# Attention by quads of heads in four column strips, with DMA transposes and engine orders planned at build time

## The chip, the cores and the metric

One core of a Trainium2 chip. The metric is device time in microseconds (us). Times are medians of several executions. Chips differ a little, so versions are compared by their ratio to the kernel before on the same chip.

## The reference, cut to what matters

```python
scores = scale * q @ k.T                      # 8 batches, 12 heads, 448 tokens, 64 wide
e = exp(scores - m)
attn = e / (sum(e) + exp(-m))                 # softmax with one more 1 in the sum
x = (attn @ v), heads side by side            # 3584 tokens x 768
h = x @ w_in                                  # 768 -> 2048, the first GEMM
g = (a0 + a1*h + a2*h^2 + a3*h^3) / (1 + |b0||h| + |b1|h^2)
out = g @ w_out                               # 2048 -> 768, the second GEMM
```

Both kernels drop the maximum `m`: the scores are small, and exp(s)/(sum exp(s) + 1) is the same number.

## The kernel before

Tokens are split 3 x 128 + 64. Heads go in pairs: a score matmul uses 64 of the 128 rows of the array, two heads beside each other; sums use 64 of 128 columns. The last 64 tokens of both heads share zero-padded blocks (`kblk`, `vblk`, `oblk`) and full-array matmuls. PE (the matmul engine) transposes q and k.

```python
def transpose_pair(b, p):                     # 8 PE transposes for a pair of heads
    for j in range(NC):
        nc.tensor.transpose(tp[:, S + j*128:S + (j+1)*128], k3[:, j, hs, :], ident)
    nc.tensor.transpose(tp[:, S + SM:S + SM + 128], kblk[b % 2][:, p, :], ident)
    # ... the same for q
    nc.vector.tensor_copy(out=qk, in_=tp)

def attend(b, p):
    for j in range(NC):                       # denominators: two strips of 64 columns
        for hh in range(2):
            r = slice(64 * hh, 64 * hh + 64)
            nc.tensor.matmul(out=den[r, 0:S], lhsT=ones, rhs=e[j][:, hh, :], ...)
    nc.tensor.matmul(out=den[:, 0:S], lhsT=oblk, rhs=e[NC], ...)   # the rest, full array
    # ... u, the numerators, in the same way from v3 and vblk

# program order: one list of work units, sorted by hand-set times
for _, f, args in sorted(work, key=lambda w: w[0]):
    f(*args)
```

A tile scheduler then adds the waits. `gemm1` and `gemm2` use the full array.

The softmax here doesn't subtract the row's maximum and nothing guards it: scores larger than these inputs give would overflow.

## Time and profile before

| | before |
|---|---|
| median time | 557.6 us (3 runs), 556.8 (4 runs beside the change) |
| profiled span | 554.7 us |
| PE, DVE, ACT busy | 502.6, 393.4, 307.9 us |
| matmuls, changes of tile shape | 3056, 528 |

DVE is the vector engine, ACT the scalar engine, POOL the GpSimd engine, which here also issues the loads; SP issues stores. A line of a view by stretches gives a stretch, its length, and the busy time and count of each engine. A timeline line gives a start, a length, an engine, a source line, the operation, and in brackets how long the engine was idle before and what ended that.

### The profile page before, as it was taken

The numbers are of one execution on the slowest core, as the hardware profiler recorded it, in microseconds if no ns is written. First come the engines' busy times: TensorE is split into PE (matmuls) and PEld (weight loads), VectorE is DVE, ScalarE is ACT, GpSimd is POOL, SyncE is SP. The second block draws the span as 40 slices with busy tenths as digits, with TensorE's granted clock in tenths as the row PEclk, the third lists the DMA queues.
The fourth block names the chain that finished last, engine by engine and source line by source line (L and its number), as shares of the span: only waits on it lengthen the run. The fifth ranks groups of instructions, "written<-read, shape, count | busy, mean of one in ns | idle before, by whom it ended". The sixth has DMA issues, their size and how long they took to land.

```text
span 554.7 us, 7452 instructions
## 1 busy us (share of the span) xinstructions
PE 502.6 (91%) x3056; PEld 237.0 (43%) x3056; DVE 393.4 (71%) x576; ACT 307.9 (56%) x353; POOL 114.2 (21%) x140
## 2 busy tenths in 40 slices
PE   2983899899999999999999999999999999877886
PEld 0331344344444444444444444444544444443443
DVE  1120399998777868778777878778777868888741
ACT  0772488867565765656565765656574765322220
POOL 9963524300610014100610014100000000000000
PEclk9987799999999999999999999999999999998899
DMA  6999999920955019510965019510000000100012
GB/s 49 81 178 172 203 174 85 95 19 30 73 59 76 30 34 97 78 28 30 70 64 75 30 33 96 79 29 30 3 27 30 30 28 30 30 28 0 30 70 73
DMA packets 113633, 34.30 MB, mean 62 GB/s; under 512 B 107200, under 2 KB 109248, under 8 KB 113600
## 3 DMA queue, kind: packets, MB, share of 16 engines
q0 software_dynamic: 109216, 22.81, 47.7%
q1 hardware_dynamic: 4384, 11.02, 5.5%
q8 instruction: 24, 0.39, 0.3%
q14 instruction: 9, 0.07, 0.0%
HBM read 45.62 MB, written 11.01 MB: 102 GB/s over the span
## 4 chain that ended last, share of the span: by engine, by line
PE 59%; DVE 27%; DMA 5%; POOL 5%; issue 2%; ACT 1%; POOLq 0%
PE hp L217 22%; PE op L277 19%; PE sps L160 5%; DVE n L247 4%; PE u L192 4%; DMA k_152<-in_k_dram 4%; DVE h L223 3%; DVE c L239 3%; DVE n L245 3%; DVE n L248 3%; DVE w L237 3%; DVE c L241 3%; PE den L183 2%; PE u L196 2%; DMA q_151<-in_q_dram 1%
## 5 line engine op out<-in xcount | busy, mean ns | idle before, releaser
L165 ACT ACTIVATE e<-sps 128x896 f16<-128x896 f32 x144 | 130.1, 916 | 144.5 <-PE sps L160 142.2
L217 PE MATMUL hp<-xt,w_in_sb 128*128 128x448 f16 x768 | 168.2, 356 | 9.9 <-DVE osb L282 5.2
L277 PE MATMUL op<-w_out_sb,g 128*128 128x384 f16 x768 | 134.5, 330 | 6.3 <-DVE h L223 3.6
L223 DVE CAST h<-hp 128x448 f16<-128x448 f32 x128 | 78.9, 621 | 45.0 <-PE hp L217 45.0
L217 PEld LDWEIGHTS <-w_in_sb 128*128 128x128 f16 x768 | 71.7, 98 | 82.5 <-issue 27.8
L277 PEld LDWEIGHTS <-g 128*128 128x128 f16 x768 | 75.2, 99 | 61.6 <-issue 10.8
L242 ACT ACTIVATE c<-c,oneeps_c 128x1792 f16<-128x1792 f16 x32 | 57.1, 1784 | 48.2 <-DVE c L241 48.1
L282 DVE COPY osb<-op 128x384 f32<-128x384 f32 x56 | 31.0, 554 | 47.4 <-PE op L277 47.3
L151 DVE COPY qk<-tp 128x960 f16<-128x960 f16 x48 | 31.1, 652 | 37.5 <-PE tp L149 37.4
L160 PE MATMUL sps<-qk 64*128 64x448 f16 x288 | 53.0, 369 | 1.8 <-DVE qk L151 1.4
L243 ACT ACTIVATE c<-c 128x1792 f16<-128x1792 f16 x32 | 54.2, 1693 | 0.2
L183 PE MATMUL den<-e,ones 128*64 128x448 f16 x288 | 43.0, 368 | 2.1 <-ACT e L165 2.1
L205 DVE TENSOR_TENSOR xt<-u,rden 128x448 f16<-128x448 f32 x48 | 29.8, 621 | 20.0 <-ACT rden L202 17.4
L200 ACT ACTIVATE lden<-den,one_c 128x448 f32<-128x448 f32 x48 | 30.6, 637 | 10.5 <-PE den L187 10.3
L251 DVE TENSOR_TENSOR g<-n,c 128x1792 f16<-128x1792 f16 x32 | 34.7, 1086 | 2.1 <-ACT c L243 2.0
L172 ACT ACTIVATE er<-sps 128x448 f16<-128x448 f32 x48 | 26.1, 543 | 18.0 <-PE sps L167 18.0
L241 DVE TENSOR_TENSOR c<-c,w 128x1792 f16<-128x1792 f16 x32 | 34.7, 1084 | 0.0
L247 DVE TENSOR_TENSOR n<-n,h 128x1792 f16<-128x1792 f16 x32 | 34.6, 1083 | 0.0
L249 DVE TENSOR_TENSOR n<-n,h 128x1792 f16<-128x1792 f16 x32 | 34.6, 1081 | 0.0
L160 PEld LDWEIGHTS <-qk 64*128 64x128 f16 x288 | 13.1, 94 | 40.8 <-issue 38.6
L202 ACT ACTIVATE rden<-lden 128x448 f32<-128x448 f32 x48 | 27.8, 580 | 0.9
L270 POOL COPY gx<-g 128x1024 f16<-128x1024 f16 x4 | 4.2, 1043 | 116.4 <-DVE g L251 116.4
(146 smaller groups left out, 493.9 us busy)
## 6 DMA issues: line engine op xcount, KB each, us to landing
out_dram<-osb SPq DMA_DIRECT2D x24, 384.0 KB, 2.3
w_in_sb<-in_moe_w_in_dram POOLq DMA_DIRECT2D x1, 3072.0 KB, 19.7
w_out_sb<-in_moe_w_out_dram POOLq DMA_DIRECT2D x1, 3072.0 KB, 21.4
out_dram<-osb SPq DMA_DIRECT2D x8, 192.0 KB, 2.7
k_111<-in_k_dram POOLq DMA_DIRECT2D x9, 64.0 KB, 3.2
q_109<-in_q_dram POOLq DMA_DIRECT2D x9, 64.0 KB, 3.2
v_112<-in_v_dram POOLq DMA_DIRECT2D x3, 192.0 KB, 4.2
k_152<-in_k_dram POOLq DMA_DIRECT2D x3, 192.0 KB, 20.9
```

The source lines that it names most:

```text
L160: nc.tensor.matmul(out=sps[:, hh, 0:S], lhsT=qk[r, S + j * 128:S + (j + 1) * 128], rhs=qk[r, 0:S], start=True, stop=True,)
L165: nc.scalar.activation(out=e, in_=sps[:, :, 0:S], func=AF.Exp, scale=scale)
L183: nc.tensor.matmul(out=den[r, 0:S], lhsT=ones, rhs=e[j][:, hh, :], start=(j == 0), stop=False, skip_group_check=True,)
L217: nc.tensor.matmul(out=hp[:, 0:S], lhsT=w_in_sb[:, c, fc * 128:(fc + 1) * 128], rhs=xt[:, c, :], start=(c == 0), stop=(c == NDC - 1),)
L223: nc.vector.tensor_copy(out=hts[b][:, fc % FG, :], in_=hp[:, 0:S])
L241: nc.vector.tensor_tensor(out=c, in0=c, in1=w, op=ALU.mult)
L242: nc.scalar.activation(out=c, in_=c, func=AF.Ln, bias=oneeps_c)
L243: nc.scalar.activation(out=c, in_=c, func=AF.Exp, scale=-1.0)
L247: nc.vector.tensor_tensor(out=n, in0=n, in1=h, op=ALU.mult)
L249: nc.vector.tensor_tensor(out=n, in0=n, in1=h, op=ALU.mult)
L251: nc.vector.tensor_tensor(out=gs[b][:, gi * FG:(gi + 1) * FG, :], in0=n, in1=c, op=ALU.mult)
L277: nc.tensor.matmul(out=op[:, 0:HD], lhsT=lhs(fc), rhs=w_out_sb[:, fc, nh * HD:(nh + 1) * HD], start=(fc == 0), stop=(fc == NFC - 1),)
```

## The change

Its intent is to take work and hand-overs off PE. 448 tokens become 4 x 112, so that no remainder is left; four heads are summed side by side in strips of 32 columns; q and k of batches 1 to 7 are reordered by POOL and transposed by DMA; the output copies move from DVE to ACT; and every engine's order comes from a simulation in the kernel's own build, which picks the next operation by readiness and rank. The diff's core:

```diff
+LAT = {"PE": 0.3, "ACT": 0.2, "DVE": 0.2, "POOL": 0.2, "SP": 2.5, "DMA": 3.5}
+class Plan:                                   # ... ready(), slot(), run(): list scheduling
+        if e == "PE" and op.name[0] != self.mode:
+            op.end += 0.095
...
+    plan = Plan({
+        "PE": ("tr", "att", "mm"),
+        "ACT": ("head", "den", "acast", "osb", "e", "rat"),
+        "DVE": ("head", "cpt", "mult", "cast", "wc", "ng"),
+        "POOL": ("load",  "perm", "gx"),       # rank: loads before reorders
+        "SP": ("x", "out"),
+    })
+    PER = 4.1                                  # us a beat of two score pairs
+    T0 = 30.0                                  # from beat 12 on
...
+        def tiles(unit, half, lhs):            # sums: four strips of 32 columns
+            for j in range(J):
+                for i in range(4):
+                    nc.tensor.matmul(
+                        out=gen[unit["slot"]][32 * i:32 * i + 32, half, 0:S],
+                        lhsT=lhs(i, j), rhs=e_sb[m % NE][:, i % 2, :], ...)
...
+            def emit(src=src, mid=mid):        # POOL reorders, then SP transposes
+                    nc.gpsimd.tensor_copy(out=mid[0].bitcast(U32)[:, pr], in_=...)
+            def emit_x(mid=mid, dst=dst):
+                nc.sync.dma_start_transpose(out=dst[n % NK]..., in_=mid[0]...)
...
-    for _, f, args in sorted(work, key=lambda w: w[0]):
-        f(*args)
+    plan.run(due)
+    for op in plan.order:
+        op.emit()
```

## The prediction

> **What bounds the kernel now.** I read the page first: busy shares, then the 40 slices.
>
> ```profile
> PE 502.6 (91%) x3056; PEld 237.0 (43%) x3056; DVE 393.4 (71%) x576; ACT 307.9 (56%) x353; POOL 114.2 (21%) x140
> ...
> PE   2983899899999999999999999999999999877886
> ```
>
> PE is busy from a tenth of the span on, and no other engine is above 71%. But matmuls overlap, so a busy PE need not be one that streams data all the time. The second view is busy time by stretch (per row: length, then busy us and count of PE, PEld, DVE, ACT, POOL, then clock, DMA share, GB/s):
>
> ```profile
> 0.00:60.00 60.00, 34.68 (x194) 11.67 (x194) 9.52 (x22) 26.03 (x38) 44.62 (x64) 0.87 1.27 125
> 60.00:100.00 40.00, 38.06 (x239) 16.15 (x238) 32.36 (x46) 31.99 (x39) 15.39 (x17) 0.97 1.48 149
> 100.00:480.00 380.00, 371.35 (x2311) 177.27 (x2309) 306.21 (x444) 235.97 (x270) 52.12 (x57) 1.00 0.40 46
> 480.00:555.00 75.00, 58.54 (x318) 31.87 (x316) 45.35 (x66) 13.94 (x8) 2.08 (x2) 0.94 0.12 43
> ```
>
> There are three regimes: a start of 60 us in which PE waits for loads, 380 us at full clock with PE 98% busy, and a tail of 75 us with about 16 us of PE gaps. What PE does while "98% busy" is in the timeline of one steady stretch (start, length, engine, line, count); I read the distances between starts:
>
> ```profile
> 206.40 0.36 PE L160 MATMUL sps<-qk 64*128 64x448 f16 x2
> 206.70 1.31 PE L217 MATMUL hp<-xt,w_in_sb 128*128 128x448 f16 x6
> 207.84 0.35 PE L167 MATMUL sps<-qk 128*128 128x448 f16 x1
> 208.03 2.76 PE L277 MATMUL op<-w_out_sb,g 128*128 128x384 f16 x16
> 210.63 1.30 PE L217 MATMUL hp<-xt,w_in_sb 128*128 128x448 f16 x6
> 211.86 0.36 PE L160 MATMUL sps<-qk 64*128 64x448 f16 x2
> ```
>
> Six first-GEMM matmuls take 207.84-206.70 = 1.14 us, 0.19 each. Sixteen of the second GEMM take 2.60 us, 0.163 each. A 64-row pair costs as much as one full matmul, so its halves overlap; but from its start to the next 128-row one are 0.30 us, not 0.19: **each change of tile shape costs about 0.10 us**. From a full matmul to another full one (207.84 to 208.03) there is none. I took the median of all start distances in 100 to 480 us: 0.189 us within the first GEMM, 0.163 within the second, 0.285 from the first GEMM to scores, 4 ns inside a pair. That makes a change 0.096 us. For the attention sums:
>
> ```profile
> 104.86 0.76 PE L192 MATMUL u<-e,v_153 128*64 128x448 f16 x6
> 105.55 0.36 PE L196 MATMUL u<-er,vblk_86 128*128 128x448 f16 x1
> ```
>
> Six matmuls, two strips of 64 columns side by side, take 0.69 us with one change: (0.69-0.10)/3 = 0.197 us a step.
>
> Over the whole trace this closes. Streaming: first GEMM 768 x 0.189 = 145.2; second 896 x 0.163 = 146.0; full and half-array attention matmuls and transposes 131; together 422 us. The program order has 528 changes of tile shape: 51 us. Waits: 70 us, of which 29 in the first 60 us, 21 in the 380 steady us, 15 in the tail, the rest between 60 and 100. First matmul at 6.7 us, 5 us after the last. So PE's own sequence bounds 85% of the time; 131 + 51 us of it are attention and switching.
>
> **What the Trainium skill says.**
> - "TensorEngine Tiling (Array Packing)", Key Properties: changing the tiling mode drains TensorE. The trace agrees: 0.285 against 0.189 us.
> - "TensorE: Matmul & The Clock Gate", Part 3, Measured speedup vs the span model: a pack of tiles takes about one matmul plus 4 ns a tile, and three column strips were measured 2.38 times as fast. The trace shows the 4 ns between two 64-column strips; no run yet shows four.
> - "DMA: Bandwidth & Descriptors", Specifications: below 512 B a transfer misses line rate. The page counts 107200 of 113633 packets under 512 B.
> - "SBUF — State Buffer", Who interferes with whom: VectorE and GpSimd can lock each other out of a shared port. The trace fits: one rational step (L248) averages 0.733 us, but 0.60 in the tail, where GpSimd is idle.
>
> **The change, part by part.**
>
> PE. (a) The 448 tokens become 4 x 112, so the 64-token remainder with its zero-padded blocks goes. Scores: 24 quads x 8 row pairs = 192 x 0.193 = 37 us (before 144 pairs and 48 full ones, the same). (b) Denominator and numerator go in four 32-column strips: 1152 matmuls, 288 steps x 0.197 = 56.7 us; before 288 steps plus 96 full matmuls x 0.189 = 75. Gain 18 us, as no step carries zeros. (c) Transposes: 384 on PE become 96 for batch 0, about 4 us; before about 19, gain about 15 us. (d) The GEMMs are unchanged: 145.2 + 146.0. (e) Changes of tile shape, counted in the instruction order of the built program: 237 instead of 528, so 22.8 us instead of 51. Sum 37+56.7+4+291.2+22.8 = **412 us**, against 473: 61 us off the bounding engine.
>
> ACT. Durations from these rows:
>
> ```profile
> L165 ACT ACTIVATE e<-sps 128x896 f16<-128x896 f32 x144 | 130.1, 916 | 144.5 <-PE sps L160 142.2
> L223 DVE CAST h<-hp 128x448 f16<-128x448 f32 x128 | 78.9, 621 | 45.0 <-PE hp L217 45.0
> L200 ACT ACTIVATE lden<-den,one_c 128x448 f32<-128x448 f32 x48 | 30.6, 637 | 10.5 <-PE den L187 10.3
> ```
>
> 192 exponentials x 0.916 = 176; 24 x (0.637+0.580) = 29 instead of 58; rational 32 x (1.784+1.693) = 111; output copies move here, 28 x about 0.81 (768 elements, between 0.543 at 448 and 0.916 at 896) = 23; four casts, 4. Sum 343 us instead of 308.
>
> DVE. 60 casts of 896 at about 1.09 (0.621 plus 448 more at the slope of 0.554 to 0.621 from 384 to 448) = 65; 24 multiplies x 1.09 = 26; the rational 32 x 7.92 (sum of its nine rows) = 253; batch 0's copies 5. Sum 350 instead of 393: output and transpose copies leave it.
>
> Both lie beside PE, at about 78% of a 450 us span, so they matter by latency only.
>
> DMA and POOL. Loads are 1 KB runs, not 256 B. POOL gains 42 reorder steps, two copies each, about 46 us (from the gx copy's 1.04 us); SP gains 42 transposes of 229 KB. Both are asked for some 30 us early in the program, so hidden.
>
> Path at the start. With POOL's first memsets and small loads gone, I put the first exponential at 10.5 us (before 14.0). Batch 0 is then ACT-bound: 24 x 0.916 + 3 x 1.22 = 25.6 us, then 2 us for the last quad: first GEMM at about 38 us, before at 60. Until then PE does transposes, scores, sums, about 19.5 us. So 38 + (412-19.5) = 430.5 us if PE never waits again. To that, chosen rather than read: 3 us while batch 1's attention limits PE; 7 us in the steady part (before: 21 in 380; fixed planned orders and fewer hand-overs take most); 5 us in the tail (before 15):
>
> ```profile
> 527.39 1.80 ACT c L242
> 529.22 1.71 ACT c L243
> 530.95 1.10 DVE g L251
> ...
> 532.10 17.25 PE op L277 x104
> ```
>
> This serial rational of the last group remains, but the plan puts a tile of the batch before ahead of it and half the casts on ACT. Then 4.5 us for the last copy and store. Span 450; the measured time was 2.9 us over the span: **453 us**.
>
> **The rivals.**
> 1. *The strips do not overlap.* Four strips halve the weight width and double weight loads per step (8 instructions in 0.2 us instead of 4). If a step took 0.25 us: 15 us more, 468; if strips ran only in pairs: 57 more, 510. For: no run shows four. Against: two show a 4 ns offset, the plan allows 0.77 us for 16.
> 2. *The fixed order turns jitter into waits.* Each engine runs a plan made with constants; a slow step, such as DVE locked out by POOL's 46 us of new copies, holds all behind it. Against: DVE and ACT keep 20% slack. At the old steady 5.6% of waits: 14 us more, 467.
> 3. *A new wait for the transposes.* If reorder plus DMA transpose took over 30 us, scores would wait each quad; 5 us each over 21 quads is 100 us. Against: steady DMA share is 0.40.
> 4. *PE is no longer the bound.* Then nothing under about 343 us counts; ACT and DVE are too far away.
> 5. *Better than I chose:* no steady waits and a first GEMM at 30 us gives about 437.
>
> **Range and chances.** Rivals 1 and 2 in mild form reach 475, rival 5 sets 438. Faster by over 2% means under 546.4 us; only rival 3, or 1 and 2 at their worst together, gets there: 0.96, 0.03, 0.01.
>
> **What would show each step.** PE start distances: 0.19 us per four-strip step, 0.10 at changes; the PE stream from the first GEMM to the end; first GEMM near 38 us; ACT busy near 343, DVE near 350; score matmuls waiting for an SP transpose would show rival 3; PE gaps ended by DVE or ACT above 7 us in the steady part rival 2. The prediction is wrong if a four-strip step exceeds 0.25 us, or if PE waits over 45 us in all.

## The result and the profile after

483.5 us (481.3 to 486.4, 4 runs) against 556.8 for the kernel before on that chip: ratio 0.8685 (95% interval 0.8639 to 0.8732). A ratio is the mean time of one kernel's fast runs over that of the other's of the same rounds, so it is not quite the ratio of the medians. Faster, as forecast; but 30 us slower than the 453 predicted and outside the range (438 to 475).

The page after, busy shares and the slices of PE:

```profile
PE 433.8 (90%) x3296; PEld 210.0 (44%) x3296; DVE 335.0 (70%) x389; ACT 319.8 (67%) x337; POOL 123.0 (26%) x186
...
PE   3873977897998999999999999999999999998985
```

PE is at 90% again, of a shorter span; its holes lie in the first ten slices, about 120 us. By stretches (start, then to 100 us, steady part, tail):

```profile
0.00:60.00 60.00, 39.29 (x353) 18.36 (x354) 14.11 (x28) 31.47 (x39) 30.56 (x53) 0.91 1.22 181
60.00:100.00 40.00, 32.33 (x258) 13.40 (x256) 30.05 (x34) 31.90 (x35) 17.80 (x23) 0.87 0.94 130
100.00:380.00 280.00, 271.02 (x2104) 128.12 (x2103) 222.75 (x250) 209.88 (x223) 72.29 (x108) 1.00 0.52 84
380.00:480.00 100.00, 91.12 (x587) 50.15 (x584) 68.14 (x80) 46.51 (x42) 2.35 (x2) 0.99 0.15 44
```

From 60 to 100 us PE is now busy for 32 of 40 us, where before it was 38, and the clock granted is 0.87. A piece of the steady part, to be set beside the timeline of before:

```profile
252.08 0.82 PE L569 MATMUL gen<-w_out,g 128*128 128x384 f16 x4
252.83 1.70 PE L417 MATMUL gen<-e,vn 112*32 112x448 f16 x32
254.46 0.82 PE L569 MATMUL gen<-w_out,g 128*128 128x384 f16 x4
255.22 0.59 PE L391 MATMUL sps<-qt,kt 64*112 64x448 f16 x4
255.74 3.42 PE L569 MATMUL gen<-w_out,g 128*128 128x384 f16 x20
```

The 32 numerator matmuls of a quad take 254.46-252.83 = 1.63 us with the change of shape after them: eight steps of four at 0.19 us. Two score pairs take 0.52, with one change.

**Where the time went.** I split every start distance between matmuls into streaming (the durations of the prediction), 0.096 us where the tile shape changes, and the rest, called waits, in which slow clock is included.

| us | before | after | predicted after |
|---|---|---|---|
| streaming | 422 | 388 | 389 |
| changes of shape (528, 237) | 51 | 23 | 23 |
| waits, with the time ahead of the first matmul and after the last | 82 | 69 | 38 |
| span | 555 | 480 | 450 |

Of the 75 us gained in the span, 34 are streaming, 28 changes of shape and 13 waits. PE's work is as predicted to within 2 us, and the error is in the waits. For streaming this agreement is partly by construction, as the split takes the prediction's durations. What checks them are the medians of start distances in the steady part: 0.189 us in the first GEMM, 0.163 in the second, 0.19 per four-strip step, mostly 0.093 to 0.096 more at a change of shape. One term is missed: the second score pair of a block starts 0.23 us after the first, not 0.193; 56 such pairs in the steady part are 2 us, counted as waits here.

| waits, us | predicted | measured |
|---|---|---|
| up to the first GEMM (forecast at 38, seen at 46.6) | 18.5 | 30.2 |
| from there to 100 us (batch 1's attention) | 3 | 16.1 |
| steady part, 100 to 380 us | 7 | 13.6 |
| tail, and after the last matmul | 9.5 | 8.7 |

What PE stood at is in the timeline of PE, and in its waits summed by cause (who <- whom: us in all, times, longest):

```profile
35.75 1.87 PE L417 MATMUL gen<-e,vn 112*32 112x448 f16 x32
45.68 1.00 PE L391 MATMUL sps<-qt,kt 64*112 64x448 f16 x4 [8.05 <-DMA qt<-qp]
46.61 1.30 PE L481 MATMUL gen<-x,w_in 128*128 128x448 f16 x3
```

```profile
PE sps L391 <- DMA qt<-qp: 11.0, 2, 8.1
```

Batch 0's attention is over by 37.6 us. PE then stands 8.05 us for the first DMA-transposed queries. The first GEMM, whose input DVE has finished by 38.8 us, has its place in the order behind those scores. The issuing queues in the same stretch:

```profile
29.95 0.70 POOL L282 DMA_DIRECT2D w_in<-in_moe_w_in_dram  x1 [0.52 <-DMA w_in<-in_moe_w_in_dram]
...
30.65 0.74 POOL L345 COPY kp<-kn 112x256 uint32<-112x256 uint32 x2
...
31.33 0.74 POOL L345 COPY qp<-qn 112x256 uint32<-112x256 uint32 x2
31.42 1.32 SPq L351 DMA_TRANSPOSE kt<-kp  x1
...
32.80 4.65 SPq L351 DMA_TRANSPOSE qt<-qp  x1
```

The reorder of batch 1's first keys comes right after the last of twelve weight loads in POOL's queue, at 30.65 us, though the trace has these keys landed at 22.3. The transposes are issued at 31.4 and 32.8 and land at 41.8 and 45.6, ten and thirteen us later, while weights are in flight. The view of the tile `qt` gives the range (smallest, median, largest):

```profile
DMA to landing us min/median/max: 3.0/3.5/17.0
```

The 17 us are those of the second queries, issued at 46.5 us beside the second GEMM's weights; the plan takes 2.5 us for every transpose.

### The profile page after: what moved, and what is told of

Same layout as the page of the kernel before. It is cut to its first block, busy times and chain, and to the rows that moved or that the text cites. A ratio compares the mean times of both kernels' runs of the same rounds, so it can differ in the third digit from the quotient of the medians.

```text
span 479.5 us, 7892 instructions
## 1 busy us (share of the span) xinstructions
PE 433.8 (90%) x3296; PEld 210.0 (44%) x3296; DVE 335.0 (70%) x389; ACT 319.8 (67%) x337; POOL 123.0 (26%) x186
## 4 chain that ended last, share of the span: by engine, by line
PE 58%; DVE 15%; ACT 11%; DMA 10%; issue 4%; POOL 1%; DVEq 0%; POOLq 0%; ACTq 0%
PE gen L569 24%; PE gen L481 19%; PE gen L417 8%; PE sps L391 6%; ACT e L397 5%; DMA w_in<-in_moe_w_in_dram 4%; DMA qt<-qp 4%; DVE h L498 3%; DVE g L519 3%; DVE n L515 2%; ACT c L533 2%; DMA kt<-kp 2%; DVE n L519 2%; DVE c L519 2%; ACT c L530 1%
## 5 line engine op out<-in xcount | busy, mean ns | idle before, releaser
L397 ACT ACTIVATE e<-sps 112x896 f16<-112x896 f32 x192 | 166.5, 922 | 83.5 <-PE sps L391 82.9
L481 PE MATMUL gen<-x,w_in 128*128 128x448 f16 x768 | 161.3, 357 | 3.8 <-ACT o L579 1.5
L569 PE MATMUL gen<-w_out,g 128*128 128x384 f16 x768 | 134.2, 326 | 2.7 <-DVE g L519 2.3
L481 PEld LDWEIGHTS <-w_in 128*128 128x128 f16 x768 | 71.3, 98 | 83.4 <-issue 25.4
L498 DVE CAST h<-gen 128x896 f16<-128x896 f32 x60 | 64.9, 1086 | 49.5 <-PE gen L481 48.8
L391 PE MATMUL sps<-qt,kt 64*112 64x448 f16 x384 | 65.0, 395 | 21.2 <-DMA qt<-qp 11.0
L438 DVE TENSOR_TENSOR x<-gen,lden 128x896 f16<-128x896 f32 x24 | 26.1, 1086 | 35.7 <-PE gen L417 35.7
L519 DVE TENSOR_TENSOR g<-n,c 128x1792 f16<-128x1792 f16 x32 | 35.0, 1095 | 21.2 <-ACT c L533 20.5
L515 DVE TENSOR_SCALAR n<-n,abc 128x1792 f16<-128x1792 f16 x64 | 45.2, 706 | 1.2
L417 PE MATMUL gen<-e,vn 112*32 112x448 f16 x768 | 43.1, 368 | 1.0 <-ACT lden L430 0.9
L345 POOL COPY qp<-qn 112x256 uint32<-112x256 uint32 x42 | 27.6, 686 | 14.7 <-DMA qt<-qp 12.2
## 6 DMA issues: line engine op xcount, KB each, us to landing
w_out<-in_moe_w_out_dram POOLq DMA_DIRECT2D x4, 768.0 KB, 20.1
```

What stands on the lines that cost most here:

```text
L345: nc.gpsimd.tensor_copy(out=mid[0].bitcast(U32)[:, pr], in_=src[n % NN].bitcast(U32)[:, 2 * pr:2 * pr + 2] .rearrange("p e j d -> p j e d"))
L391: nc.tensor.matmul(out=sps[m % NS][0:P, hh, 0:S], lhsT=kt[n % NK][r, pr, j, :], rhs=qt[n % NK][r, pr].rearrange("p j c -> p (j c)"), start ...
L397: nc.scalar.activation(out=e_sb[m % NE], in_=sps[m % NS][0:P, :, 0:S], func=AF.Exp, scale=scale)
L417: nc.tensor.matmul(out=gen[unit["slot"]][32 * i:32 * i + 32, half, 0:S], lhsT=lhs(i, j), rhs=e_sb[m % NE][:, i % 2, :], start=(j == 0), st ...
L438: nc.vector.tensor_tensor(out=x_sb[b % NX][:, 2 * qd:2 * qd + 2, :], in0=gen[un_u["slot"]][:, :, 0:S], in1=r, op=ALU.mult)
L481: nc.tensor.matmul(out=gen[unit["slot"]][:, f // 2, 0:S], lhsT=w_in_sb[gi][:, c // 2, c % 2, (fc % FG) * 128:(fc % FG + 1) * 128], rhs=x_s ...
```

## The experiments

**Theory.** The loss at the start is the DMA transposes: reordered late, landing late behind weight loads, and, as orders are fixed, ready GEMM work standing behind them. **Rivals**: ACT's pace or the loads would set the start anyway; the low clock after the long wait is the loss; the plan's own pace holds attention back. In the table, spans and first GEMMs (us from the span's start) are of the profiled runs; the ratios are to the kernel before in the same rounds. Only pe_b1, wout_late and plan_knows ran on the control's chip. The change itself had ratios of 0.8685 and 0.8644, which the intervals allow, so differences across chips are sure to about 2 us only. Executions of one kernel differ by up to 5 us in span (479.5 to 484.6 for the change), so small differences are read from ratios.

| run | edit | ratio (95%) | span, us | first GEMM |
|---|---|---|---|---|
| change itself, again | none | 0.8644 (0.8613 to 0.8674) | 479.7 | 47.9 |
| pe_b1 | batch 1 transposed on PE | 0.8500 (0.8471 to 0.8529) | 473.1 | 40.5 |
| wout_late | second weights later | 0.8622 (0.8594 to 0.8650) | 475.9 | 48.0 |
| plan_knows | plan told of 11 us | 0.8571 (0.8543 to 0.8598) | 475.9 | 41.1 |
| wout_perm | wout_late, reorders first | 0.8510 (0.8471 to 0.8550) | 468.9 | 39.9 |
| warm | needless matmuls in the wait | 0.8648 (0.8612 to 0.8684) | 480.9 | - |
| pace_only | faster pace | 0.8548 (0.8514 to 0.8581) | 475.3 | - |
| pace | wout_perm and faster pace | 0.8251 (0.8221 to 0.8282) | 459.2 | 40.4 |
| pace_win | pace, other order of loads | 0.8251 (0.8226 to 0.8276) | 459.6 | - |
| all_pe | all transposes on PE | 0.9103 (0.9066 to 0.9140) | 504.1 | - |
| more_changes | 214 more changes of shape | 0.8979 (0.8942 to 0.9015) | 497.3 | - |
| more_full | its control | 0.8739 (0.8704 to 0.8774) | 485.3 | - |
| strips_serial | strips head by head | one run | 483.1 | - |
| extra_one | 12 more matmuls in one strip | one run | 525.6 | - |
| extra_spread | the same over four strips | one run | 487.5 | - |

All results were correct. A dash: not listed.

### The start: the control, batch 1 on PE, later weights, a plan that knows

> The changed kernel itself, for comparison on this chip. Both theories: 0.868 of the kernel before, span about 479.5 us, PE waits of 8 us and 3 us for transposed queries near 38 to 46 us and near 61 to 64 us.

As expected: 482.1 us, with waits of 8.6 and 3.5 us for the transposed queries.

```diff
-        if b == 0:
+        if b <= 1:
             transpose_by_pe(n)
```

> Batch 1 is transposed on PE too, so its score matmuls wait for no DMA transpose behind the weights. Theory A (late DMA transposes at the start cost about 15 us, through two waits, a lowered clock and attention that falls behind): the waits near 38 and 61 us go, the first GEMM starts near 38 us instead of 46.6, PE gains 4 to 5 us of work, the span falls to 466 to 472 us. Theory B (the start is bound by ACT's pace and by loads anyway): the first GEMM still starts after 44 us and the span stays at 480 us or grows by the 4 us.

473.9 us, span 6.6 us down although PE got more to do; the first GEMM at 40.5. The waits for DMA transposes are gone from PE. So they bound the start, not ACT's pace or the loads of weights. The profiled span is 1 us above the 466 to 472 expected (the four executions: 470.6 to 473.1): PE now stands 6.6 us, up to 77.5, for a DVE cast, so something else holds the stretch after 60 us.

```diff
+            if n in (7, 8):                   # in attention(n), after loads(n)
+                for cg in (2 * n - 14, 2 * n - 13):
+                    w_out_ops.append(w_out_op(cg))
-    w_out_ops = [w_out_op(cg) for cg in range(NG)]
+    w_out_ops = []
```

> The 3 MB of the second GEMM's weights are asked for some 20 to 35 us later, after the loads of quads 7 and 8. Theory A: transposes issued from 42 us on land in about 5 us instead of 12 to 17, the second wait goes and the first shrinks by 2 to 4 us; span 470 to 475 us. Theory B: 479 us as before.

480.3 us; the ratio lies inside the interval of the control, so no gain is shown. In the traces the second pair of transposes now lands in 4.4 and 6.6 us instead of 12.5 and 17, and the wait near 63 us is gone, but the first pair still lands at 42.9 and 47.0. It is issued beside the first weights, and the first GEMM stays at 48.0. PE stands 5.0 us for transposes instead of 12.1, but batch 0 ends later (see the section on the clock); what took up the rest is not shown.

```diff
+SLOW = ("xk3", "xq3", "xk4", "xq4", "xk5")
-            t = max(t, d.land if d.land else d.end + LAT[d.eng])
+            lat = 11.0 if d.name in SLOW else LAT[d.eng]
+            t = max(t, d.land if d.land else d.end + lat)
```

> Nothing is moved in memory; only the plan is told that the first five transposes land 11 us after issue instead of 2.5, so that PE's order puts first-GEMM matmuls ahead of the late scores. Theory A': the harm is done by the fixed order (GEMM work that is ready stands behind scores that are not); first GEMM near 38 us, span 469 to 473 us. Rival: the late transposes themselves delay batch 1's attention, ACT then paces it, and the order gains at most 3 us: 476 us or more.

477.6 us, ratio 0.0073 under the control's: 4 us. The first GEMM moves to 41.1 us as the theory says, but PE then stands 7.3 us at 65.7, at the next late transpose. The span, 475.9, is at the rival's 476. The order alone recovers 4 of the 8 us that pe_b1 gains on the same chip, so the fixed order is a part of the loss and the lateness itself another; the runs do not rank them.

### Both ends of the queue: later weights and earlier reorders

```diff
-        "POOL": ("load",  "perm", "gx"),
+        "POOL": ("perm", "load", "gx"),
```

(with the edit of the later second weights)

> The later second weights of the earlier run, and besides GpSimd's reorder copies go ahead of the loads that are still waiting in its queue, so that the first transposes are issued near 24 us instead of 31. Theory A (the transposes come late because reorder and transpose stand behind weight loads): the first pair lands before 37 us, no score waits over 2 us for it, first GEMM near 39 us, span 468 to 471 us, as far down as with batch 1 transposed on PE less its 5 us of PE work. Rival (only taking the transposes off DMA helps): a wait of over 4 us stays, span 475 us.

473.0 us, span 468.9, within the theory's 468 to 471, the first GEMM at 39.9. The first keys' transpose is issued at 23.9 us instead of 31.4. It still takes 10.8 us and the queries' 14 us, so they are not faster, only asked for sooner (the expected landing before 37 us holds for the keys, 34.6, not for the queries, 39.3). What is left of PE's wait for them:

```profile
PE sps L394 <- DMA qt<-qp: 1.8, 1, 1.8
```

This is as good as taking batch 1 off DMA (0.8510 against 0.8500), without its 5 us of PE work.

### The clock

```diff
+                    if m == 24:               # ahead of the score that waits
+                        for d in range(40):
+                            nc.tensor.matmul(out=sps[m % NS][:, 0, 0:S], ...)
```

> 40 needless full matmuls (their result is overwritten at once) are put in front of the score that waits 8 us for its transpose, so PE does not sit idle there and the granted clock stays up. If the lowered clock after the wait (0.74 in 40 to 60 us) is worth what the slow matmuls after it show, nine at about 0.4 instead of 0.19 us and two score pairs, the span falls by 2 to 3 us from 479.7. Rival: the clock is most of the loss; over 6 us. Or the matmuls only add themselves: no gain.

483.0 us: no gain, as the last of the three readings has it. The Trainium skill, in "TensorE: Matmul & The Clock Gate", Part 1, says that an idle window of about 3.4 us brings the clock down to half. The trace of the change agrees: 8 us without work, then half the clock from 40.8 to 51.0 us (0.74 on average over 40 to 60). But its clock is at half once more from 88.6 to 95.4 us, and in the 3.4 us before that PE never stood for more than 0.41 us, each time for an exponential; it was busy for 1.84 of the 3.4 us. So here a half-busy stretch was enough.

The needless matmuls did keep the clock up (1.00 over 40 to 60 us). From the late score to the 24 matmuls of the first GEMM 8.57 us pass instead of the control's 9.81, so the low clock after this wait is worth about 1 us. The waits up to 60 us fell from about 25 to 19 us, but the extra matmuls took PE's time, and PE still stood 3.3 us for the next transpose at 65.5, as before (3.5): what is gained ahead of a wait that nothing shortened is lost in it. Two limits of this test: the half clock between 60 and 100 us (10.2 us of it in the change) was not touched; and in this trace, as in those of wout_late and plan_knows, the clock is at half for 6.8 us near 29 to 36 us too, and batch 0 ends 3 to 4 us later than in the control. What made it so is not shown.

### The pace

```diff
-    PER = 4.1
-    T0 = 30.0
+    PER = 3.9
+    T0 = 22.0
```

> On top of the run with later second weights and earlier reorders, the pace constants of the plan: 3.9 us a beat instead of 4.1, from 22 us instead of 30, so that batch 1's attention may go ahead of the first batch's first GEMM. Theory: half of the waits left between 60 and 200 us (about 20 us there) come from attention that the plan holds back to a pace slower than PE; they fall by 6 to 12 us, span 457 to 463 us. Rival: ACT, at 80% in that stretch, or the late loads pace it whatever the plan asks; 467 us or more.

460.3 us, ratio 0.8251, in the expected 457 to 463: 13 us below the run without the pace edit, and the best version. **It beats the change by 4.5%** (0.8251/0.8644). By stretches:

```profile
0.00:60.00 60.00, 42.56 (x414) 19.29 (x414) 18.16 (x32) 38.79 (x48) 32.83 (x57) 0.97 1.25 164
60.00:100.00 40.00, 35.79 (x280) 16.02 (x283) 39.44 (x46) 35.03 (x36) 17.02 (x25) 1.00 1.10 160
100.00:380.00 280.00, 278.95 (x2200) 131.41 (x2192) 223.76 (x251) 213.69 (x230) 68.01 (x104) 1.00 0.55 85
```

PE is busy 279 of 280 us in the steady part (before this edit 273, in the change 271), and the waits there are 4.0 us instead of 13.6. Without the pace edit they were 11.9, so 8 us of these "steady" waits were a plan that asks for attention later than PE could use it, not jitter. From the first GEMM to 100 us waits are 9.5 us, in the change 16.1.

> The two pace constants alone, on the changed kernel. If late transposes and pace are separate losses: 5 to 10 us under 479.7. If attention that is asked for earlier only waits longer for transposes behind the weights: no gain, the waits for transposed queries near 40 and 62 us grow.

477.0 us, 0.0096 under the control, 5 us: both readings are partly right. The steady waits shrink, but the waits for transposed queries grow from 8.6 and 3.5 us to 8.7 and 7.8. The two losses overlap: the pace is worth 5 us behind late transposes and 13 us without them.

```diff
     w_in_ops.append(w_in_op(1))
-    w_in_ops.append(w_in_op(2))
     loads(4)
-    w_in_ops.append(w_in_op(3))
+    w_in_ops.append(w_in_op(2))
     loads(5)
+    w_in_ops.append(w_in_op(3))
```

> On top of the best run so far (later second weights, earlier reorders, faster pace) the first weights are asked for in the order weights 1, loads 4, weights 2, loads 5, weights 3, so that quads 4 and 5 come sooner. Two waits for transposes of 2 us each are left there. If the queue of loads ahead of them is their cause: they go, span 454 to 457 us. If first-GEMM weights come too late then, or what is left is jitter and ACT's pace at the start: 458 to 461 us, no gain.

460.9 us, no gain: a miss. The order of these loads is not what is left.

### Was the gain where the prediction put it?

The transposes back on PE for all batches (`b < B` in place of `b == 0`):

> Every batch is transposed on PE: the part 'DMA transposes' undone. 672 more transposes at 45 ns a start distance (batch 0 in the trace of the change) = 30 us, and 69 more changes of tile shape at 0.096 us = 7 us, less the 8 us of late transposes at the start: span about 508 us, ratio to the kernel before 0.915. If PE were not the bound in the steady part, the span would grow by less than 10 us.

505.9 us; span 504.1, expected 508, but near by luck: the 45 ns were read in batch 0, and in the steady part a block of 16 transposes takes 0.52 us with its change of shape, 26 ns each or 18 us in all; and the 8 us of late transposes did not come back, as PE's transposes now wait 20.1 us for loads of queries (7.0 in the change). By the ratios (0.0459 x 557) DMA transposes are worth some 25 us to this version even with their late start, as PE is the bound.

The price of a change of shape, by tiny matmuls of one data column ahead of each first-GEMM group, of another shape or of the full one:

```diff
+                if f % 2 == 0:
+                    nc.tensor.matmul(
+                        out=gen[unit["slot"]][0:32, f // 2, 480:481], lhsT=ones[:, :],
+                        rhs=ones[:, 0:1], start=True, stop=True, ...)
```

> 128 tiny matmuls of another tile shape (128 rows x 32 columns, one data column) are put before the first-GEMM groups; the program order then has 451 changes of tile shape instead of 237. If a change costs 0.096 us on the bounding engine: 214 x 0.096 = 20.5 us and 128 x about 0.03 us for the matmuls, span about 503 us. Rival: changes cost PE nothing when there is slack elsewhere; under 490 us.

> The control: the same 128 tiny matmuls in the full tile shape, so that the number of changes stays 237. Only the matmuls' own time is added, 128 x 0.03 to 0.1 us: span 482 to 492 us. The difference to the run with other shapes is the price of 214 changes.

The control costs 0.0095 (5 us), the other shape 0.0335 (19 us): 0.0240 x 557 = 13 us for 214 changes, 0.06 us each instead of 0.096. The two timelines, first with other shapes, then the control:

```profile
249.92 1.31 PE L485 MATMUL gen<-x,w_in 128*128 128x448 f16 x6
251.16 0.18 PE L481 MATMUL gen<-ones 128*32 128x1 f16 x1
251.27 1.31 PE L485 MATMUL gen<-x,w_in 128*128 128x448 f16 x6
```

```profile
250.34 1.29 PE L485 MATMUL gen<-x,w_in 128*128 128x448 f16 x6
251.47 0.17 PE L481 MATMUL gen<-ones,ident 128*128 128x1 f16 x1
251.50 0.73 PE L485 MATMUL gen<-x,w_in 128*128 128x448 f16 x3
```

Into the other shape 1.24 us pass instead of 1.13, out of it 0.11 instead of 0.03; by medians 0.094 and 0.081 us more. So PE does pay what the prediction says, less a little on the way out. Summed over all tiny matmuls PE pays 15 us more than in the control from 60 us on. That the net price is less, 13 us, because a part falls where PE would have stood anyway, is argued, not shown. Rival "slack elsewhere hides it" falls.

The strips, first by another order of the same matmuls:

```diff
-            for j in range(J):
-                for i in range(4):
+            for i in range(4):
+                for j in range(J):
```

> The four strips of a step are issued one head after the other instead of side by side, the same matmuls otherwise. If strips overlap only when neighbours differ in strip: 1152 matmuls at 0.19 us instead of 288 steps at 0.2: 160 us more on the bounding engine, span 620 to 650 us. If the overlap came from elsewhere: 480 us.

484.9 us: no loss. My expectation was wrong: a denominator block of 16 takes 0.90 us to the next start instead of 0.87. Either strips have nothing to do with it, or each strip takes its own matmuls in turn whatever the order of issue. Two more runs tell these apart:

```diff
+            for x in range(12):               # ahead of each denominator block
+                i = 0                         # extra_one;  x % 4 in extra_spread
+                nc.tensor.matmul(out=gen[un_d["slot"]][32 * i:32 * i + 32, 0, 0:S], ...)
```

> Ahead of each of the 24 denominator blocks 12 needless matmuls are added, all in strip 0 (overwritten by the real ones). If a strip takes one matmul at a time: 24 x 12 x 0.187 = 54 us more on PE, span 525 to 535 us. If strips do not matter and four matmuls always run side by side: 13 us, span 493 us.

> The same 12 needless matmuls, dealt out over the four strips. If strips work side by side: 3 steps x 24 x 0.197 = 14 us, span 492 to 496 us. If they do not: 54 us as in the run with one strip.

Blocks with 12 more in strip 0 take 3.13 us instead of 0.87, 0.188 us for each; dealt over four strips 1.44 us, 0.19 for each four. The times, 527.4 and 489.2 us, are 45 and 7 us above the 482.1 of the change, less than 54 and 14; these are single runs on another chip, and the readings rest on the start distances. So strips do work side by side, one matmul at a time in each, and the order of issue within a block hardly matters. The trace of extra_one shows how: three real matmuls of the other strips start at 255.26 us, ahead of the last two needless ones of strip 0 (255.44 and 255.63), which stand before them in the program.

## Why the prediction was wrong, point by point

- **PE's sum, 412 us: right,** as far as the medians above check it. Streaming was 388 and changes 23, 411 together. Four strips take 0.19 us a step (I took 0.197), and a change of shape lengthens a start distance by 0.08 to 0.096 us.
- **ACT 343, DVE 350 us: a little high, 320 and 335.** The durations were right (an exponential 0.922 us, I took 0.916), but neighbours overlap in the records, so count times mean is more than busy time: 192 x 0.922 = 177 against 166.5 here. Neither was the bound, as said. The row of the exponentials:

```profile
L397 ACT ACTIVATE e<-sps 112x896 f16<-112x896 f32 x192 | 166.5, 922 | 83.5 <-PE sps L391 82.9
```

- **"Both are asked for some 30 us early in the program, so hidden": the step that failed**, with its consequence "first GEMM at about 38 us". For the first quads after batch 0 there are no 30 us: the reorder stood behind weight loads until 30.65 us, the transposes landed 10 to 17 us after issue, and the GEMM had its place behind them. Measured: first GEMM at 46.6 us, and 30.2 us of waits up to it instead of 18.5. With the reorders first and the second weights later it is 39.9, and the span is 11 us down. The other half of that step, batch 0 bound by ACT up to 38 us, was right: the GEMM's input was finished at 38.8. Rival 3 of the prediction was this wait; I spoke against it with the DMA share of the kernel before in its steady part, 0.40, but the wait is in the start, where the same view showed 1.27.
- **"3 us while batch 1's attention limits PE": mis-sized, 16.1 us.** It was chosen, not worked out. Late transposes and the plan's pace, which I did not use, make it; pace and earlier transposes bring it to 9.5.
- **"7 us in the steady part": mis-sized, 13.6 us.** The pace edit leaves 4.0, so the 7 would have been fair without a pace slower than PE.
- **Tail 5 and end 4.5 us: right**, 3.4 and 5.3. The 2.9 us from span to time set one execution's span against the median of others; in each execution of the record it is 1.7 to 2.0 us.
- **A reading: "0.60 in the tail".** That is a piece of the chain that ended last; the step L248 itself takes 0.68 us there. The sense holds: over the kernel before it takes 0.68 us where GpSimd is idle (23 of 32) and 0.87 on average where GpSimd works (9).
- **Rival 1** (no overlap of strips) falls by the two runs with more matmuls. **Rival 2** (jitter of the fixed order) falls as the main cause: with orders fixed in the same way, at another pace, the steady waits fall to 4.0 us.

The two repairs take 20.5 us of span off, of the 30 us that the prediction missed. The other 10 us stay open: in the best version 24 us are idle or slow before the first GEMM, in part because ACT gives out batch 0's exponentials 0.8 us apart (scores wait 5.8 us for ACT in the whole trace), and in part two waits of 2 us for transposes that still land 9 to 14 us after issue. Nothing here separates those further.

On the transposes, "DMA: Bandwidth & Descriptors", Queues, rings and completion order, says that each DMA engine goes round the queues that have work, a packet at a time. A transpose of many small packets beside weight loads would then advance slowly. The trace has 37632 packets of 256 B on SP's queue, 896 for each of the 42 transposes, and the long landings, but no run varied the packets, so this is argued, not shown.

## What to carry to other kernels

Count the bounding engine's work from start distances and changes of shape: that part of the forecast held here, to about 2 us of 412. Then walk through the start of the changed program queue by queue, since a lead that holds in the steady part does not exist there, and a fixed order makes one late transfer stop everything behind it. When an order is planned from constants, compare their latencies and pace with the trace first: moving one kind of load and the reorder copies, and changing two numbers, gained 22 us here, against 75 us by the whole rewrite.

## What the Trainium skill lacked or had wrong

- "TensorEngine Tiling (Array Packing)", Key Properties, says that a mode change drains TensorE but gives no figure: 0.094 us into a 32-column shape and 0.081 us out of it were measured here; at 0.096 us each 237 of them are 23 us of PE's 480.
- "TensorE: Matmul & The Clock Gate", Part 3, has a measured speedup of column strips alone for three only, 2.38. Four strips of 112 rows ran at 0.19 us for four matmuls of 448 columns, where one strip took 0.188 for one: practically fourfold.
- "TensorE: Matmul & The Clock Gate", Part 3, says that matmuls start and end strictly in program order. The starts here do not: in extra_one matmuls of other strips start at 255.26 us, before earlier ones of the busy strip at 255.44 and 255.63. So strips need not alternate in the order of issue (0.90 against 0.87 us for 16 matmuls).
- "DMA: Bandwidth & Descriptors" gives a bandwidth for DMA transposes, 261 GB/s in one kernel, but no time to landing for one between on-chip buffers: in the change about 3 us at the least and up to 17.0 us beside weight loads, for 229 KB.
- "TensorE: Matmul & The Clock Gate", Part 4, gives 275 to 390 ns for one PE transpose of 128 x 128, but no spacing in a stream: in the kernel before one starts 0.056 us after another, and in all_pe 16 of 112 x 64 took 0.52 us together with the change of shape, so 0.03 us each.
